# Seven low-half subtractions per token span placed elsewhere in VectorE's order

## The chip, the cores and the metric

The kernel runs on one core of a Trainium2 chip. The metric is device time in microseconds (us) of one execution; the time before is the median of three runs. The engines are called as in the profile: PE (TensorE), DVE (VectorE), ACT (ScalarE), POOL (GpSimd), SP (SyncE, which issues most DMAs). PEld is PE's weight load.

## The reference, cut to what matters

The input is 4 sequences of 3008 tokens of 256 numbers. A two-dimensional Fourier transform is taken of each, its real part is kept, and two feed-forward layers follow:

```
x = fft(fft(x, axis=1), axis=2).real      # (12032, 256)
h = x @ w_in1 ; x = relu(h)**2 @ w_out1   # 256 -> 2048 -> 256
h = x @ w_in2 ; y = (h * cos(h)) @ w_out2 # 256 -> 2048 -> 256
```

All is wanted in float32 precision, so each operand of a product is kept as two parts, a rounded high half and the low half that is left (value minus high half), and a product is three matmuls: low weight by high token, high weight by low token, high by high.

## The kernel before, in words

The Fourier transform and layer 1 fill the first 880 us or so; the change does not touch them. Layer 2 follows, and is cut into 12 spans of token pairs (`SPANS`, L45; index k), 11 of 512 columns and a last one of 388. For each span there are 8 steps (`NS`, L673; index i), each of which makes two of the 16 groups of 128 hidden units and adds what they give to the output.

**Operands of the first product.** It is done as a two by two block product with seven multiplications instead of eight. So each span needs seven token operands, named at L679: B11, B22 and B21 are columns of the layer's input as loaded; T1X, T2X, T3X and T4X are differences of such columns, made in place by `diff` (L691, on POOL for every span but the first). For each operand `x_hi` (L696, ACT) writes the rounded high half and `x_lo` (L702, DVE) the low half: one subtraction of 128x512 with both inputs in SBUF, listed by the profile at L704. The seven operands of span k are prepared while span k-1 is computed, and are kept in ten rotating buffers.

**One step.** The seven products M1 to M7 (L706) of three matmuls each go to two accumulation banks. M1, M6, M7 and M4 use bank 0, M5, M3 and M2 bank 1. Between them, sums are taken out: M1's result is copied by ACT (x1, L730), then M6 is added to the bank, that sum is copied by DVE (x2, L732), then M7 is added, and so on; so M6 must wait until x1 has read the bank, and M7 until x2 has. The corners C11, C12, C22 (DVE, listed at L237) and C21 (ACT, L742) make the hidden values h of the two groups. For each group j of the two: n (ACT, L747) rounds h to whole turns into the bank pp, r (DVE, L751) takes the rest, c (ACT, L757) the cosine, g (first group on DVE, second on POOL at L762) multiplies by h, `l2_hi` (ACT, L768) makes the high half and `l2_lo` (POOL, L773) the low half of the result. Then the 24 matmuls of the second product (m0 to m7, L785) add them to the output. Both n write the same bank pp, so n2 waits until r1 has read it.

**The order** is written out by hand. Every piece is given a time by `at` (L81), all pieces are sorted by it, and the sorted list is issued; each engine then runs its own part of the list strictly in that order. The unit of the table `OFF` (L983) is a step: the pieces of step i of a span stand at i + OFF, so a fraction tells the place within a step. By these numbers DVE's order within every step is r2 (.177), x2 (.362), C12 (.447), g1 (.513), C11 (.635), C22 (.701), x5 (.827), r1 (.893), and POOL's is l2 (.075), a `diff` where there is one (.5), g2 (.567), l1 (.818). PE's M3 stands at .133, M6 at .267, M7 at .467. ACT's n2 is at .052, x1 at .154, c1 at .321.

The lists `hi`, `lo` and `dif` (L994 to L996) give the places of the operands of span k, counted in steps of span k-1: for instance B11's low half at 3.76 stands in step 3 between C22 and x5. The first span's operands have a list of their own (L998 to L1002).

A step is told in the prediction by M3's start; it is recognised in the trace as the first of the three matmuls `b<-x,wel` of a step (M3, M6, M7 in this order).

Of the kernel before, what the change touches and what calls it, by code (L numbers as in the profile page):

```python
# [74 lines left out]
class Order:  # L75
# [5 lines left out]
    def at(self, t, fn, name=None):  # L81
        self.ops.append((TIMES.get(name, t), len(self.ops), fn))
# [12 lines left out]
def kernel(ctx: ExitStack, tc: tile.TileContext, x, x128, cs, tab0, tab1, w_in1, w_out1, w_in2, w_out2, out):  # L95
# [583 lines left out]
    T1X, B11, B22, T2X, T3X, B21, T4X = range(7)  # L679

    def load_o(k):
        c, w = SPANS[k]
        o_in[k] = [buf(t, "oin") for t in ("A0", "A1")]
        for t, o in zip(o_in[k], o_dram):
            nc.sync.dma_start(out=t[:, :, :w], in_=o[:, :, c:c + w])
# [5 lines left out]
    def diff(k, j, e):  # L691

        a, b = {T1X: ("b12", B11), T3X: (B22, "b12"), T2X: (B22, T1X), T4X: (B21, T2X)}[j]
        e.tensor_tensor(out=cols_of(k, j), in0=cols_of(k, a), in1=cols_of(k, b), op=ALU.subtract)

    def x_hi(k, j):  # L696
        tag = XTAGS[(7 * k + j) % 10]
        x = buf(tag, "x", F32R, late["pool"] if tag in ("cv", "xc") else work, XTAGS.count(tag))[:, :, :SPANS[k][1]]
        right[k, j] = x
        nc.scalar.activation(x[:, 0], cols_of(k, j), AF.Copy)  # L700

    def x_lo(k, j):  # L702
        x = right[k, j]
        nc.vector.tensor_tensor(out=x[:, 1], in0=cols_of(k, j), in1=f32(x)[:, 0], op=ALU.subtract)  # L704
# [3 lines left out]
    def product(k, i, b, pair_of, start):  # L708
        w = SPANS[k][1]
        j, r = pair_of  # L710
        (wh, wl), x = left(j, i), right[k, r]
        for q, (st, mv) in enumerate(((wl, 0), (wh, 1), (wh, 0))):
            nc.tensor.matmul(bank["b"][b][:, :w], st, x[:, mv], start=start and q == 0, stop=q == 2, skip_group_check=True)  # L713
# [4 lines left out]
    def ends(k, i):  # L718
        return k == len(SPANS) - 1 and i == NS - 1

    def copy_of(k, i, x, b, e):
        w = SPANS[k][1]
        if x == 5:
            u = buf("mid", "x5", F32, late["pool"], 2, (P, BLK)) if k == i == 0 else buf("u2", "x5", shape=(P, BLK))
        else:
            u = buf("zb", "x", bufs=2, shape=(P, BLK))
        us[k, i, x] = u = u[:, :w]
        src = bank["b"][b][:, :w]
        if e is nc.scalar:
            nc.scalar.activation(u, src, AF.Copy)  # L730
        else:
            nc.vector.tensor_copy(u, src)  # L732
# [6 lines left out]
    def corner(k, i, j, n, b, x):  # L739
        src, dst = bank["b"][b][:, :SPANS[k][1]], h_of(k, i, j)[:, n]  # L740
        if x is None:
            nc.scalar.activation(dst, src, AF.Copy)  # L742
        else:
            tt(dst, src, us[k, i, x], ALU.add)
# [25 lines left out]
    def l2_lo(k, i, j):  # L770
        hi, r = gs[2, k, i, j], rs.pop((k, i, j))
        lo = (buf("B1", "gl", F32R) if j and i % 2 else gl_buf())[:, :, :SPANS[k][1]]
        (V if ends(k, i) else G).tensor_tensor(out=lo, in0=r, in1=f32(hi), op=ALU.subtract)  # L773
        gs[2, k, i, j] = hi, lo

    def l2_mm2(k, i, n):
        m, j, half = n // 4, n // 2 % 2, n % 2
        w = SPANS[k][1]
        if i == 0 and j == half == 0:
            accs[2, k, m] = ps_a.tile([P, 2, BLK], F32, name=f"acc{m}")  # L780
        f = 2 * i + j
        hi, lo = gs[2, k, i, j]
        for q in range(3 * half, 3 * half + 3):
            part, g = ((0, hi), (1, hi), (0, lo))[q // 2]
            nc.tensor.matmul(accs[2, k, m][:, q % 2, :w], w_out_t([c[part] for c in wo2], f, m), g[:, q % 2],  # L785
                             start=f == 0 and q < 2, stop=f == NF - 1 and q >= 4)

    def l2_out(k, m):
        c, w = SPANS[k]
        a = accs.pop((2, k, m))[:, :, :w]  # L790
        last = k == len(SPANS) - 1
        o = buf("A0" if last and m else "B0", "y")[:, :, :w]
        dst = out[m].rearrange("p (n w) -> p n w", n=2)[:, :, c:c + w]
        if last:
            nc.scalar.activation(o[:, 0], a[:, 0], AF.Copy, scale=2.0 * math.pi)
            o2 = buf("zb", "y", bufs=2, shape=(P, BLK))[:, :w]
            nc.vector.tensor_scalar(out=o2, in0=a[:, 1], scalar1=2.0 * math.pi, scalar2=None, op0=ALU.mult)
            nc.scalar.dma_start(out=dst[:, 0], in_=o[:, 0])
            nc.sync.dma_start(out=dst[:, 1], in_=o2)
            return  # L800
        if m == 0:
            nc.scalar.activation(o, a, AF.Copy, scale=2.0 * math.pi)
        else:
            nc.vector.tensor_scalar(out=o, in0=a, scalar1=2.0 * math.pi, scalar2=None, op0=ALU.mult)
        nc.sync.dma_start(out=dst, in_=o)
# [183 lines left out]
    for k in range(len(SPANS)):  # L989
        base = L2S + STEP * NS * k  # L990
        if k:
            prev = base - STEP * NS
            at(prev + 2.1 * STEP, lambda k=k: load_o(k))
            hi = {B11: 2.82, B22: 3.82, T1X: 4.82, T2X: 6.82, T3X: 7.3, B21: 7.82, T4X: 8.3}  # L994
            lo = {B11: 3.76, B22: 4.76, T1X: 5.76, T2X: 7.32, T3X: 7.76, B21: 8.32, T4X: 8.34}
            dif = {T1X: 4.5, T3X: 5.5, T2X: 6.5, T4X: 7.5}  # L996
            t = {j: [prev + STEP * v[j] if j in v else None for v in (dif, hi, lo)] for j in range(7)}
        else:  # L998
            at(T2S - 13, lambda k=k: load_o(k))
            hi = {B11: 0, B22: 1, T1X: 2, T3X: 3, T2X: 4, B21: 5, T4X: 6}  # L1000
            dif = {T1X: 1, T3X: 2, T2X: 3, T4X: 4}
            t = {j: [T2S - 9.53 + dif.get(j, 0), T2S - 9.55 + hi[j], T2S - 8.55 + hi[j]] for j in range(7)}  # L1002
        for j in range(7):
            if j in dif:
                at(t[j][0], lambda k=k, j=j: diff(k, j, G if k else V))
            at(t[j][1], lambda k=k, j=j: x_hi(k, j))
            at(t[j][2], lambda k=k, j=j: x_lo(k, j))
        for i in range(NS):
            ops = {"M1": lambda k, i: product(k, i, 0, M1, True), "M6": lambda k, i: product(k, i, 0, M6, False),
                   "M7": lambda k, i: product(k, i, 0, M7, False), "M4": lambda k, i: product(k, i, 0, M4, False),  # L1010
                   "M5": lambda k, i: product(k, i, 1, M5, True), "M3": lambda k, i: product(k, i, 1, M3, False),
                   "M2": lambda k, i: product(k, i, 1, M2, True),
                   "x1": lambda k, i: copy_of(k, i, 1, 0, A), "x2": lambda k, i: copy_of(k, i, 2, 0, V),
                   "x5": lambda k, i: copy_of(k, i, 5, 1, V),
                   "C11": lambda k, i: corner(k, i, 0, 0, 1, 1), "C12": lambda k, i: corner(k, i, 0, 1, 1, 2),
                   "C21": lambda k, i: corner(k, i, 1, 0, 0, None), "C22": lambda k, i: corner(k, i, 1, 1, 0, 5)}
            for j in range(2):
                for n, fn in (("n", l2_n), ("r", l2_r), ("c", l2_cos), ("g", l2_g), ("h", l2_hi)):
                    ops[f"{n}{j + 1}"] = lambda k, i, j=j, fn=fn: fn(k, i, j)
                ops[f"l{j + 1}"] = lambda k, i, j=j: l2_lo(k, i, j)  # L1020
            for n in range(8):
                ops[f"m{n}"] = lambda k, i, n=n: l2_mm2(k, i, n)
            for name, fn in ops.items():
                off = END.get(name, OFF[name]) if ends(k, i) else OFF[name]
                at(base + STEP * (i + off), lambda k=k, i=i, fn=fn: fn(k, i), (name, k, i))
        for m, n in ((0, "m3"), (1, "m7")):
            off = END[n] if k == len(SPANS) - 1 else OFF[n]
            at(base + STEP * (NS - 1 + off + 0.09), lambda k=k, m=m: l2_out(k, m))
# [117 lines left out]
```

## Time and profile before

| what | value |
|---|---|
| median of 3 runs | 1907.06 us (1906.25 to 1907.62) |
| the profiled execution, its own time | 1904.97 us |
| its span (first to last instruction) | 1902.9 us |
| PE busy | 1836.1 us, 96% |
| DVE, ACT, POOL busy | 1454.8, 1443.0, 1374.1 us (76%, 76%, 72%) |
| mean granted TensorE clock | 0.996 of full speed |

What lies around the span is 2 us, and the profiled execution is 2 us below the median. Busy shares are averages over stages that differ. In layer 2 PE is the engine with the least idle time, so the way to read it is PE's order in time: how long a step takes, which steps take longer than others, and what PE waited for in those.

### The profile page before, as it was taken

To read this page: it belongs to the slowest core of one execution; us is meant where nothing else is said; L and a number is where in the kernel's file an instruction comes from. 1 tells how busy PE (TensorE), PEld (TensorE's weight loads), DVE (VectorE), ACT (ScalarE), POOL (GpSimd) and SP (SyncE) were. 2 spreads that over 40 slices of the span, in tenths; PEclk is the share of its full clock that TensorE was granted. 3 is DMA by queue.
4 is the path that set the end of the run, shared out by engine and by line. 5 is a ranking of instruction groups with operands and counts; after the bars stand their busy time and mean duration, and the time that the engine had idled before them with its cause. 6 is when DMAs were issued, how large, how long until landed. Compare 5 with 4: busy or idle time off the path is not lost.

```text
span 1902.9 us, 23618 instructions
## 1 busy us (share of the span) xinstructions
PE 1836.1 (96%) x8256; PEld 1507.2 (79%) x8256; DVE 1454.8 (76%) x1867; ACT 1443.0 (76%) x1618; POOL 1374.1 (72%) x1144
## 2 busy tenths in 40 slices
PE   6899999999999999999999999999999999999998
PEld 3678787788888888887777777787777777787788
DVE  6889958768578886776777787877777777777775
ACT  3788777878788988887777777777777777777776
POOL 1567777778777778776768786777777777777775
PEclk9899999999999999999999999999999999999999
DMA  8563434244243343442110101010010101010000
GB/s 281 179 248 107 148 117 149 104 142 147 96 124 117 104 137 105 121 149 90 65 45 1 44 1 45 1 45 21 24 45 1 45 1 45 0 45 28 12 23 17
DMA packets 72410, 153.17 MB, mean 80 GB/s; under 512 B 8304, under 2 KB 31872, under 8 KB 72196
## 3 DMA queue, kind: packets, MB, share of 16 engines
q1 hardware_dynamic: 69732, 143.46, 22.7%
q0 software_dynamic: 1840, 6.73, 1.2%
q8 instruction: 64, 1.05, 0.2%
q10 hardware_dynamic: 720, 1.50, 0.2%
q14 instruction: 54, 0.44, 0.1%
HBM read 105.20 MB, written 51.09 MB: 82 GB/s over the span
## 4 chain that ended last, share of the span: by engine, by line
PE 63%; DVE 8%; issue 5%; ACT 3%; POOL 3%; DVEq 0%; ACTq 0%; POOLq 0%
PE b L713 18%; PE acc L785 18%; PE acc L644 18%; PE h L602 8%; DVE r L751 3%; DVE h L237 2%; POOL gl L773 2%; ACT pp L747 2%; DVE x L732 1%; PE h L335 1%; DVE x L704 1%; POOL r L762 1%; ACT x L730 1%; DVE s L237 0%; DVE u L609 0%
## 5 line engine op out<-in xcount | busy, mean ns | idle before, releaser
L632 POOL TENSOR_TENSOR gl<-s,gh 128x256 fp32r<-128x256 f32 (+2 forms) x768 | 601.3, 815 | 211.7 <-ACT gh L622 169.5
L773 POOL TENSOR_TENSOR gl<-r,gh 128x1024 fp32r<-128x1024 f32 (+1 forms) x190 | 454.1, 2396 | 58.8 <-ACT gh L768 57.7
L762 POOL TENSOR_TENSOR r<-r,h 128x1024 f32<-128x1024 f32 (+1 forms) x95 | 225.3, 2372 | 204.1 <-ACT r L757 183.5
L751 DVE SCALAR_TENSOR_TENSOR r<-pp,h 128x1024 f32<-128x1024 int32 (+1 forms) x192 | 229.5, 1195 | 112.4 <-ACT pp L747 108.7
L619 ACT ACTIVATE s<-s 128x1024 f32<-128x1024 f32 (+2 forms) x192 | 199.7, 1040 | 86.4 <-DVE s L237 82.1
L785 PE MATMUL acc<-gh,wbl 128*128 128x512 f32 (+1 forms) x768 | 264.7, 385 | 0.0
L768 ACT ACTIVATE gh<-r 128x1024 fp32r<-128x1024 f32 (+1 forms) x192 | 200.0, 1042 | 82.8 <-DVE r L237 82.7
L237 DVE TENSOR_TENSOR s<-u,h 128x512 f32<-128x512 f32 (+2 forms) x380 | 240.0, 673 | 25.0 <-POOL gl L632 3.5
L644 PE MATMUL acc<-gh,wbh 128*128 128x512 f32 (+2 forms) x768 | 236.9, 390 | 0.7 <-DVE o L669 0.7
L644 PE MATMUL acc<-gl,wbh 128*128 128x512 f32 (+2 forms) x768 | 235.4, 387 | 1.5 <-POOL gl L632 1.3
L785 PE MATMUL acc<-gh,wbh 128*128 128x512 f32 (+1 forms) x768 | 233.8, 385 | 1.0 <-ACT gh L768 1.0
L644 PE MATMUL acc<-gh,wbl 128*128 128x512 f32 (+2 forms) x768 | 234.4, 386 | 0.0
L785 PE MATMUL acc<-gl,wbh 128*128 128x512 f32 (+1 forms) x768 | 233.5, 385 | 0.4 <-POOL gl L773 0.4
L713 PE MATMUL b<-x,wah 128*128 128x512 f32 (+1 forms) x768 | 233.6, 385 | 0.0
L747 ACT ACTIVATE pp<-h 128x1024 int32<-128x1024 f32 (+1 forms) x192 | 192.1, 1000 | 52.3 <-DVE r L751 50.2
L609 DVE SCALAR_TENSOR_TENSOR u<-zb,wc,h 128x512 f32<-128x512 f32 (+2 forms) x190 | 138.9, 731 | 95.7 <-PE h L602 94.9
L622 ACT ACTIVATE gh<-s 128x1024 fp32r<-128x1024 f32 (+2 forms) x192 | 201.0, 1047 | 6.1
L620 ACT ACTIVATE s<-s 128x1024 f32<-128x1024 f32 (+2 forms) x192 | 200.9, 1046 | 6.1
L237 DVE TENSOR_TENSOR h<-b,x 128x512 f32<-128x512 f32 (+1 forms) x288 | 187.0, 677 | 18.7 <-PE b L713 15.0
L732 DVE COPY x<-b 128x512 f32<-128x512 f32 (+1 forms) x192 | 129.9, 676 | 84.7 <-PE b L713 84.6
L713 PE MATMUL b<-x,weh 128*128 128x512 f32 (+1 forms) x576 | 175.5, 386 | 0.0
L757 ACT ACTIVATE pp<-r,halfpi 128x1024 f32<-128x1024 f32 (+1 forms) x96 | 106.1, 1105 | 83.0 <-DVE r L751 83.0
(145 smaller groups left out, 3420.7 us busy)
## 6 DMA issues: line engine op xcount, KB each, us to landing
oin<-o SPq DMA_DIRECT2D x22, 512.0 KB, 5.2
y_out<-y SPq DMA_DIRECT2D x22, 512.0 KB, 3.1
inT<-x_in SPq DMA_DIRECT2D x18, 512.0 KB, 8.6
o<-o SPq DMA_DIRECT2D x16, 512.0 KB, 3.7
mid<-w_in SPq DMA_DIRECT2D x14, 511.5 KB, 5.8
mid<-w_out SPq DMA_DIRECT2D x14, 511.0 KB, 4.3
t<-tab SPq DMA_DIRECT2D x9, 756.0 KB, 4.4
t<-tab SPq DMA_DIRECT2D x9, 752.0 KB, 6.9
```

The source lines that it names most:

```text
L237: nc.vector.tensor_tensor(out=out, in0=in0, in1=in1, op=op)
L620: nc.scalar.activation(s[:, :, :w], s[:, :, :w], AF.Square)
L622: nc.scalar.activation(hi[:, :, :w], s[:, :, :w], AF.Copy)
L632: nc.gpsimd.tensor_tensor(out=lo[:, n, cols], in0=s[:, n, cols], in1=f32(hi)[:, n, cols], op=ALU.subtract)
L644: nc.tensor.matmul(accs[1, k][m][:, n, :w], wt, g[:, n, :w], start=begin and i == 0, stop=end and i == 2)
L713: nc.tensor.matmul(bank["b"][b][:, :w], st, x[:, mv], start=start and q == 0, stop=q == 2, skip_group_check=True)
L747: nc.scalar.activation(bank["p"].bitcast(I32)[:, :, :SPANS[k][1]], hs[k, i, j], AF.Copy, bias=0.25)
L751: nc.vector.scalar_tensor_tensor(out=r, in0=bank["p"].bitcast(I32)[:, :, :SPANS[k][1]], scalar=-1.0, in1=hs[k, i, j], op0=ALU.mult, op1=AL ...
L762: (V if ends(k, i) else G).tensor_tensor(out=r, in0=r, in1=h, op=ALU.mult)
L768: nc.scalar.activation(hi, rs[k, i, j], AF.Copy)
L773: (V if ends(k, i) else G).tensor_tensor(out=lo, in0=r, in1=f32(hi), op=ALU.subtract)
L785: nc.tensor.matmul(accs[2, k, m][:, q % 2, :w], w_out_t([c[part] for c in wo2], f, m), g[:, q % 2], start=f == 0 and q < 2, stop=f == NF - ...
```

## The change

One line of the table of places is replaced: that of the low halves of the operands of span 1 and later. No instruction is added or removed, and no size, buffer or transfer is changed.

```diff
             hi = {B11: 2.82, B22: 3.82, T1X: 4.82, T2X: 6.82, T3X: 7.3, B21: 7.82, T4X: 8.3}
-            lo = {B11: 3.76, B22: 4.76, T1X: 5.76, T2X: 7.32, T3X: 7.76, B21: 8.32, T4X: 8.34}
+            lo = {B11: 3.34, B22: 4.34, T1X: 5.34, T2X: 7.34, T3X: 7.96, B21: 8.34, T4X: 8.35}
             dif = {T1X: 4.5, T3X: 5.5, T2X: 6.5, T4X: 7.5}
```

## Rows read from the trace of the kernel before

**Rows 1.** The page's part on engines: busy us, share of the span, instructions.
```profile
PE 1836.1 (96%) x8256; PEld 1507.2 (79%) x8256; DVE 1454.8 (76%) x1867; ACT 1443.0 (76%) x1618; POOL 1374.1 (72%) x1144
```

**Rows 2.** Waits of PE, 915 to 1830 us: releaser, total us, times, longest.
```profile
PE b L713 <- ACT x L730: 19.4, 32, 0.6
PE b L713 <- DVE x L732: 2.9, 11, 0.3
```

**Rows 3.** Timeline of PE, some starts: start us, us, instruction [idle before <-releaser].
```profile
1004.16 0.39 PE L713 MATMUL b<-x,wel 128*128 128x512 f32 x1
...
1014.36 0.39 PE L713 MATMUL b<-x,wel 128*128 128x512 f32 x1
...
1016.50 0.50 PE L713 MATMUL b<-x,wel 128*128 128x512 f32 x1 [0.62 <-ACT x L730]
...
1025.49 0.39 PE L713 MATMUL b<-x,wel 128*128 128x512 f32 x1
...
1057.01 0.39 PE L713 MATMUL b<-x,wel 128*128 128x512 f32 x1
...
1059.15 0.50 PE L713 MATMUL b<-x,wel 128*128 128x512 f32 x1 [0.62 <-ACT x L730]
...
1068.76 0.39 PE L713 MATMUL b<-x,wel 128*128 128x512 f32 x1
```

**Rows 4.** Timelines of POOL and DVE around three low halves in the places of before.
```profile
1010.12 2.40 POOL L773 TENSOR_TENSOR gl<-r,gh 128x1024 fp32r<-128x1024 f32 x1
...
1010.32 2.75 DVE L704 TENSOR_TENSOR x<-oin,x 128x512 fp32r<-128x512 f32 x1
...
1021.45 1.07 DVE L704 TENSOR_TENSOR x<-oin,x 128x512 fp32r<-128x512 f32 x1
...
1265.42 0.74 DVE L704 TENSOR_TENSOR x<-oin,x 128x512 fp32r<-128x512 f32 x1
```

**Rows 5.** The chain that ended last, 1013 to 1017 us: start us, us, what.
```profile
1013.00 0.68 DVE x L732
1013.67 1.14 DVE r L751
...
1014.90 1.03 ACT pp L747
1015.93 0.52 ACT x L730
...
1016.50 0.96 PE b L713 x3
```

**Rows 6.** Timelines of DVE, POOL and ACT, 1296 to 1304 us, between two even steps.
```profile
1298.39 1.21 DVE L751 SCALAR_TENSOR_TENSOR r<-pp,h 128x1024 f32<-128x1024 int32 x1
1301.03 1.22 DVE L751 SCALAR_TENSOR_TENSOR r<-pp,h 128x1024 f32<-128x1024 int32 x1 [1.42 <-ACT pp L747]
1302.17 0.88 DVE L704 TENSOR_TENSOR x<-oin,x 128x512 fp32r<-128x512 f32 x1
1303.22 0.69 DVE L732 COPY x<-b 128x512 f32<-128x512 f32 x1 [0.17 <-PE b L713]
...
1296.75 2.40 POOL L773 TENSOR_TENSOR gl<-r,gh 128x1024 fp32r<-128x1024 f32 x1
1300.09 2.42 POOL L773 TENSOR_TENSOR gl<-r,gh 128x1024 fp32r<-128x1024 f32 x1 [0.94 <-ACT gh L768]
1302.46 1.75 POOL L694 TENSOR_TENSOR oin<-oin 128x512 f32<-128x512 f32 x1
...
1299.91 1.02 ACT L747 ACTIVATE pp<-h 128x1024 int32<-128x1024 f32 x1
```

**Rows 7.** Timeline of DVE: x2 of two steps, and two low halves in a row.
```profile
1017.50 0.69 DVE L732 COPY x<-b 128x512 f32<-128x512 f32 x1 [0.24 <-PE b L713]
...
1059.82 1.28 DVE L704 TENSOR_TENSOR x<-oin,x 128x512 fp32r<-128x512 f32 x2
1061.02 0.68 DVE L732 COPY x<-b 128x512 f32<-128x512 f32 x1
```

## The prediction

> **What bounds the kernel now.** I read the engines' busy times first: PE is busy 96% of the span, the others about three quarters [rows 1]. So only time in which PE stands still can be won. Next, PE's waits in layer 2 from the point where the moved instructions begin: M6 waited for x1 (ACT's copy of M1) 32 times, 19.4 us, and M7 for x2 (DVE's copy) 11 times, 2.9 us [rows 2]. Nothing else shows there. What such a wait costs is read from step lengths, since a stopped PE also starts again more slowly. Step 3 of this span, from M3 to M3, takes 1014.36 - 1004.16 = 10.20 us without a wait; step 4, whose M6 waited 0.62 us, takes 1025.49 - 1014.36 = 11.13 us [rows 3]. So one M6 stall costs 0.93 us, not 0.62. Step 0 of the next span, in which M6 and then M7 waited, takes 1068.76 - 1057.01 = 11.75 us [rows 3]: 0.62 us more.
>
> Why M6 waits is in the chain of work that ended last. It runs x5, r1, n2, x1, M6 with no gap to speak of: DVE's copy at 1013.00, r1 at 1013.67, ACT's n2 at 1014.90, x1 at 1015.93, PE at 1016.50 [rows 5]. In front of that x5 stands B11's low half. It takes 2.75 us, from 1010.32 to 1013.07, and POOL had begun a subtraction of 2.40 us at 1010.12, 0.20 us earlier [rows 4]. That one ended at 1012.52; the low half ended 0.55 us later. Its work is therefore about 0.6 us, and the other 2.2 us is standing still behind POOL. Where POOL did not stand in the way, the same instruction took 0.74 us [rows 4].
>
> The low half of B22 in the next step takes 1.07 us [rows 4] and no M6 stall follows. In all, 32 low halves of 2.6 to 2.75 us stand in the trace of DVE from 915 us on (three per span for 11 spans, less one), and as many M6 waits [rows 2]: one for one. In the span in which B11 took 0.74 us [rows 4], no wait follows it.
>
> The Trainium skill ("SBUF — State Buffer", section "SBUF: two separate sides") says that VectorE and GpSimd share a pair of ports, which an instruction of either holds to its end; for VectorE that holds for instructions with two SBUF inputs. The trace agrees: 2.75 us is POOL's remainder plus 0.55.
>
> **What the change does, part by part.** No work is added or removed, and `x_lo` issues no DMA, so no queue is touched.
>
> T2X (7.32 to 7.34), B21 (8.32 to 8.34) and T4X (8.34 to 8.35): no other DVE piece stands between old and new place (r2 is at .177, x2 at .362). DVE's order is the same, so these 33 of the 77 cost nothing by themselves.
>
> B11, B22 and T1X go from behind C22 to between r2 and x2, 33 instructions. The trace already has an instruction in that place: T2X. In the one span where it follows a step without a wait, r2 starts at 1301.03 and T2X at 1302.17, taking 0.88 us; x2 behind it still waits 0.17 us for PE [rows 6]. POOL is not idle there: its l2 runs from 1300.09 to 1302.51 [rows 6]. But only the last 0.3 us of it are left when DVE arrives, against 2.2 us in the old place. So the price in the new place is zero as long as x2 is not late, and what is queued behind is x2, then C12 and g1; M7 waits for x2. How late x2 may be is worked out from step 0: there x2 starts 1061.02 - 1059.15 = 1.87 us after M6, and in step 4 1017.50 - 1016.50 = 1.00 us after it, when only PE held it [rows 3, 7]. It was 0.87 us late and that cost 0.62 us, so 0.25 us are free. Bounds for one such place: nothing below, since x2 cannot go before PE is done; above, a full block as in the old place, ending 2.75 us after 1302.17, which makes x2 1.7 us late. I take zero, from the nearest row, T2X.
>
> With these three gone from the old place, x5 waits only for PE, r1 is early, and n2 starts when ACT is free. The even step shows it: r1 is done at 1299.60 and n2 starts at 1299.91 without a wait [rows 6].
>
> T3X goes from 7.76 to 7.96, between r1 and r2, 11 instructions. In the even step r1 ends at 1299.60, POOL's l1 ended at 1299.15 and its l2 starts at 1300.09, after 0.94 us in which POOL waited for ACT; r2 starts at 1301.03, after 1.42 us of waiting for n2 [rows 6]. A low half of 0.6 to 0.7 us fits: from 1299.6 to 1300.2. It may hold l2 back by 0.1 us. Above, the bound is a block by the whole of l2 (a rival below). I take zero on DVE.
>
> Step 0, with B21 and T4X in a row before x2: today r2 of that step is late because of T3X, and both take 1.28 us unblocked [rows 7]. Afterwards r2 ends at the even step's time and they meet the end of l2. l2 then ends at about 1302.6; B21 ends 0.54 us behind it (as T2X did: 1303.05 against 1302.51 [rows 6]), T4X 0.6 us later, at 1303.75, where x2 could have started at 1303.22. So x2 is some 0.55 us late, 0.25 are free, and the step pays about 0.3 us instead of today's 0.62. Bounds: nothing, or today's 0.62.
>
> **The sum.** 32 M6 stalls x 0.93 = 29.8 us, and 11 x (0.62 - 0.3) = 3.5 us: 33 us in all. Against the profiled execution's 1904.97 us that is 1872; the median of the runs is 2 us above that execution, so I say **1874 us**. If every stall went, it would be 29.8 + 11 x 0.62 = 36.6 us, or 1870.5. That is the floor: every step then takes 10.20 us, the time of its 45 matmuls.
>
> **Rivals.**
>
> *POOL's difference goes first.* At 4.5 and 5.5 POOL has a `diff` queued right behind l2, at the very place where B22 and T1X now wait. If it takes the ports, the low half waits another 1.2 us (the `diff` of 1.75 us at 1302.46 was itself held 0.54 us by T2X [rows 6]), x2 is 1.0 us late and 22 steps pay 0.75 us: 17 us back, 1891. Against it: T2X stands before the `diff` of T4X in the same way, and DVE went first. By the Trainium skill (the same section) whoever starts first holds the ports; it does not say who is served first of two that wait.
>
> *T3X is caught by l2.* If l1 ends after 1300, l2 starts at once and T3X waits for it until 1303.05; r2 ends at 1304.3, then the two low halves, so x2 starts 2.3 us late and the step pays 2.05 us instead of 0.3: 11 x 1.75 = 19 us back, 1893. Against it: the 0.94 us in which POOL waits for ACT [rows 6].
>
> *The stall stays or moves.* If n2 or x1 were held by something else as soon as r1 is early, most of the gain would be missing: about 1905. Against it stand the even steps. That the change doesn't do what it says belongs here: POOL is not idle at .34, only nearly done.
>
> *Slower.* POOL needs some 8.5 of each 10.20 us (2.41 for g2, 2.4 each for l1 and l2, 1.3 for a `diff`). If, in steps that follow each other without stalls, its l2 came to start after r2's end, 2.1 us later than in rows 6, every low half before x2 would stand a full 2.75 us: x2 1.7 us late, 1.45 us paid, 33 times, 48 us; step 0 pays 1.4 us more than today, 15 us; less the 30 won, that is 33 us slower, 1940. It decides from a low half of some 2.2 us on, where 33 late x2 cost what 32 stalls do. Against it: l2's start is set by ACT's high half, not by POOL's backlog [rows 6].
>
> **How the numbers follow.** Forecast 0.77, `diff` first 0.08, T3X caught 0.06, stall stays 0.05, slower 0.04. From the floor to the second rival is 0.91; the range 1870 to 1893 takes in these cases and leaves 0.09 out. Without the two rivals the forecast's own range is 1870 to 1878. A difference of 0.2% (3.8 us) is about what a measurement of this kernel can tell from none. Faster by more than that: the first three cases and a part of the fourth, 0.93; within it 0.03; slower 0.04.
>
> **What would show it.** Right: low halves of at most about 1.1 us each; no M6 wait on ACT's copy; steps of 10.20 us, 10.5 for step 0; M7's wait on x2 shorter than 0.3 us; `diff` some 0.5 us longer behind B22 and T1X. Wrong: low halves of 2 us or more in their new places, x2 without a wait for PE in front of it, M7 waits in steps 3 to 5, or r2 late in step 0.

## The result and the profile after

The changed kernel took 1871.24 us, the median of 4 runs (1870.84 to 1872.39), against 1906.65 us for the kernel before, the median of its 4 runs (1904.18 to 1907.62). The ratio is 0.9817, with a 95% interval of 0.98 to 0.9834: 1.8% or 35.4 us faster. The forecast was 1874 us, the range 1870 to 1893.

The page's first lines, on the span and on the engines, of the changed kernel:

```profile
span 1870.6 us, 23619 instructions
...
PE 1828.6 (98%) x8256; PEld 1513.5 (81%) x8256; DVE 1400.0 (75%) x1867; ACT 1437.0 (77%) x1618; POOL 1379.5 (74%) x1144
```

Against [rows 1] DVE is busy 55 us less with the same number of instructions, and POOL 5 us more. The same stretch of layer 2 as in [rows 2], 915 to 1830 us, has no wait of PE left; the busy times up to 1800 us say the same (window, its length, then busy us of PE, PEld, DVE, ACT and POOL with their instructions, granted clock of PE, DMA share, GB/s):

```profile
915.00:1800.00 885.00, 885.00 (x3905) 730.71 (x3905) 658.97 (x782) 671.97 (x782) 694.72 (x305) 1.00 0.08 26
```

PE is busy for all 885 us. The groups of the moved instruction and of POOL's differences in layer 2, those of 512 columns (line, operation and shape, count, busy us, mean ns, idle before), first in the kernel before:

```profile
L704 DVE TENSOR_TENSOR x<-oin,x 128x512 fp32r<-128x512 f32 x70 | 112.6, 1621 | 0.0
L694 POOL TENSOR_TENSOR oin<-oin 128x512 f32<-128x512 f32 x40 | 56.2, 1406 | 0.0
```

and then in the changed kernel:

```profile
L694 POOL TENSOR_TENSOR oin<-oin 128x512 f32<-128x512 f32 x40 | 65.5, 1637 | 0.0
L704 DVE TENSOR_TENSOR x<-oin,x 128x512 fp32r<-128x512 f32 x70 | 58.6, 848 | 0.0
```

A low half takes 848 ns in the mean where it took 1621. POOL's differences take 231 ns more each: part of the waiting has gone over to POOL, where it holds up nothing that PE waits for.

The timelines of the changed kernel over steps 7 and 0 (PE, then DVE, then POOL), which answer to [rows 3, 6, 7]:

```profile
1044.39 0.39 PE L713 MATMUL b<-x,wel 128*128 128x512 f32 x1
1045.75 0.39 PE L713 MATMUL b<-x,wel 128*128 128x512 f32 x1
...
1054.59 0.39 PE L713 MATMUL b<-x,wel 128*128 128x512 f32 x1
1055.95 0.39 PE L713 MATMUL b<-x,wel 128*128 128x512 f32 x1
...
1064.87 0.39 PE L713 MATMUL b<-x,wel 128*128 128x512 f32 x1
...
1045.57 0.87 DVE L704 TENSOR_TENSOR x<-oin,x 128x512 fp32r<-128x512 f32 x1
1046.62 0.69 DVE L732 COPY x<-b 128x512 f32<-128x512 f32 x1 [0.18 <-PE b L713]
...
1051.99 1.21 DVE L751 SCALAR_TENSOR_TENSOR r<-pp,h 128x1024 f32<-128x1024 int32 x1
1053.12 0.68 DVE L704 TENSOR_TENSOR x<-oin,x 128x512 fp32r<-128x512 f32 x1
1054.63 1.22 DVE L751 SCALAR_TENSOR_TENSOR r<-pp,h 128x1024 f32<-128x1024 int32 x1 [0.82 <-ACT pp L747]
1055.77 1.48 DVE L704 TENSOR_TENSOR x<-oin,x 128x512 fp32r<-128x512 f32 x2
1057.17 0.68 DVE L732 COPY x<-b 128x512 f32<-128x512 f32 x1
...
1050.35 2.42 POOL L773 TENSOR_TENSOR gl<-r,gh 128x1024 fp32r<-128x1024 f32 x1
1053.69 2.41 POOL L773 TENSOR_TENSOR gl<-r,gh 128x1024 fp32r<-128x1024 f32 x1 [0.93 <-ACT gh L768]
```

Step 7 takes 1054.59 - 1044.39 = 10.20 us, step 0 takes 1064.87 - 1054.59 = 10.28 us instead of 11.75 [rows 3]. T3X's low half at 1053.12 takes 0.68 us. POOL's l2 starts at 1053.69, 0.11 us before the recorded end of that low half, and takes its usual 2.41 us, so neither holds up the other; r2 comes when ACT lets it. The two low halves at 1055.77 make x2 start 1.22 us after M6, where it starts 0.87 us after it in step 7.

Where the time came from is counted in layer 2 itself: from M3 of step 3 of the first span to M3 of step 6 of the last one. Kernel before, PE's timeline:

```profile
919.13 0.39 PE L713 MATMUL b<-x,wel 128*128 128x512 f32 x1
...
1872.73 0.34 PE L713 MATMUL b<-x,wel 128*128 128x388 f32 x1
```

and the changed kernel:

```profile
921.85 0.39 PE L713 MATMUL b<-x,wel 128*128 128x512 f32 x1
...
1840.44 0.34 PE L713 MATMUL b<-x,wel 128*128 128x388 f32 x1
```

953.60 us against 918.59 us: 35.0 of the 35.4 us by which the medians differ. The spans of the two profiled executions differ by 32.3 us only, since that of the changed kernel reaches this stretch 2.7 us later (921.85 against 919.13); the change touches nothing before it.

### The profile page after: what moved, and what is told of

Read it like the earlier page. It is cut to its first block, busy times and chain, and to the rows that moved or that the text cites. A ratio compares the mean times of both kernels' runs of the same rounds, so it can differ in the third digit from the quotient of the medians.

```text
span 1870.6 us, 23619 instructions
## 1 busy us (share of the span) xinstructions
PE 1828.6 (98%) x8256; PEld 1513.5 (81%) x8256; DVE 1400.0 (75%) x1867; ACT 1437.0 (77%) x1618; POOL 1379.5 (74%) x1144
## 3 DMA queue, kind: packets, MB, share of 16 engines
q0 software_dynamic: 1840, 6.73, 1.2%
## 4 chain that ended last, share of the span: by engine, by line
PE 79%; DVE 2%; ACT 1%; issue 0%; ACTq 0%; DVEq 0%
PE acc L785 27%; PE b L713 24%; PE acc L644 18%; PE h L602 9%; PE h L335 1%; DVE s L237 0%; DVE u L609 0%; DVE inT L237 0%; DVE r L751 0%; ACT o L668 0%; ACT pp L747 0%; DVE ws L237 0%; DVE wf L237 0%; DVE h L237 0%; PE pp L602 0%
## 5 line engine op out<-in xcount | busy, mean ns | idle before, releaser
L644 PEld LDWEIGHTS acc<-gl,wbh 128*128 128x128 f32 x768 | 144.7, 188 | 31.3 <-POOL gl L632 3.4
```

The lines of the kernel that those rows point to most:

```text
L644: nc.tensor.matmul(accs[1, k][m][:, n, :w], wt, g[:, n, :w], start=begin and i == 0, stop=end and i == 2)
```

## The experiments

The theory: a low half that meets a running subtraction of POOL stands until that one ends, so x5, r1, n2, x1 and M6 are late, and the change takes the low halves out of that meeting. The rivals: it is only their place in DVE's order, whatever POOL does; or only some of the moves count.

**Each part alone.** `e1_t3x_back` is the changed kernel with T3X's low half in its old place:

```diff
-            lo = {..., T2X: 7.34, T3X: 7.96, ...}
+            lo = {..., T2X: 7.34, T3X: 7.76, ...}
```

> The changed kernel with T3X's low half back at 7.76; B11, B22 and T1X stay in their new places. Theory (a low half that starts behind POOL's l1 stands about 2.2 us, x5, r1, n2, x1 and M6 are late by it, one M6 stall costs 0.93 us and makes step 0 pay 0.62 us more): T3X's low half takes 2.75 us, all others at most 1.1 us; 11 M6 waits of 0.62 us; step 0 takes 11.75 us again, against 10.29 us in the changed kernel; 11 x 1.46 = 16 us over the changed kernel, 1887 us. Rival (each moved low half brings its share by its own 0.6 us of DVE time, whatever POOL does): a quarter of the gain is lost, about 9 us, 1880 us. Rival (only the first three matter, T3X's new place brings nothing): 1871 us.

It took 1886.19 us (ratio to the kernel before 0.9903, interval 0.9886 to 0.9919), 15.0 us over the changed kernel. Its PE waits, 915 to 1840 us, and its PE timeline in step 0:

```profile
PE b L713 <- ACT x L730: 6.8, 11, 0.6
PE b L713 <- DVE x L732: 2.6, 10, 0.3
```

```profile
1054.07 0.39 PE L713 MATMUL b<-x,wel 128*128 128x512 f32 x1
1056.21 0.50 PE L713 MATMUL b<-x,wel 128*128 128x512 f32 x1 [0.61 <-ACT x L730]
1058.82 0.50 PE L713 MATMUL b<-x,wel 128*128 128x512 f32 x1 [0.28 <-DVE x L732]
1065.80 0.39 PE L713 MATMUL b<-x,wel 128*128 128x512 f32 x1
```

11 M6 waits, step 0 of 11.73 us, and no wait in any other step from step 3 of the first span on: the theory's numbers, and neither rival's.

`e2_t3x_only` is the kernel before with that one low half moved:

```diff
-            lo = {..., T2X: 7.32, T3X: 7.76, ...}
+            lo = {..., T2X: 7.32, T3X: 7.96, ...}
```

> The kernel before with T3X's low half alone moved to 7.96. Theory: 21 of the 32 M6 waits stay (those behind B11 and T1X), those of step 0 go, and with them its longer M7 wait; 16 us under the kernel before, 1890.5 us, and the two parts of the change add up: this gain and that of the other three together make the whole 35 us. Rival (the stalls are linked, so that taking one out of a span moves POOL's subtractions into the way of others, as in the one span of the trace before where B22 was blocked instead of B11 and T1X): the number of blocked low halves per span stays 3 or changes to other operands, and the gain is under 10 us.

It took 1889.28 us (ratio 0.9918, interval 0.9904 to 0.9933), 16.0 us under the kernel before on the same chip (1905.29). The PE wait left in it:

```profile
PE b L713 <- ACT x L730: 12.6, 21, 0.6
```

21 waits, as expected, and no M7 wait. The parts add up: T3X 16.0 us here, the other three 1905.29 - 1886.19 = 19.1 us, together 35.1 of the 35.4 us.

**Is it POOL, or the place?** In `e3_l1_memset` nothing is moved; POOL's l1 is replaced.

```diff
-        (V if ends(k, i) else G).tensor_tensor(out=lo, in0=r, in1=f32(hi), op=ALU.subtract)
+        if j or ends(k, i):
+            (V if ends(k, i) else G).tensor_tensor(out=lo, in0=r, in1=f32(hi), op=ALU.subtract)
+        else:
+            G.memset(f32(lo), 0.0)
```

> The kernel before, all low halves in their places of before, but POOL's l1 (low half of the first group's result, two inputs read from SBUF) is a memset of the same tile; the output lacks that low half. Theory (the low half stands because POOL's instruction reads SBUF beside it): low halves in the old places of 0.6 to 0.8 us, no M6 wait behind them, layer 2's steps 10.2 to 10.3 us, about 1871 to 1874 us with nothing moved. Rival (any POOL instruction holds the ports to its end, a writing one too): the low half lasts until the memset ends and 0.55 us more, so what is left of the stall goes with the memset's length. Rival (it is the place in DVE's order, not POOL): M6 waits of 0.6 us stay, 1905 us.

It took 1869.7 us, one run, with all low halves in their old places, and its layer 2 has no PE wait. POOL's memset and the low half of B11, from the timelines of POOL and DVE:

```profile
1006.10 0.96 POOL L776 MEMSET gl<- 128x1024 f32 x1
...
1006.42 0.68 DVE L704 TENSOR_TENSOR x<-oin,x 128x512 fp32r<-128x512 f32 x1
```

The low half starts 0.32 us into the memset and still takes 0.68 us. So the place alone costs nothing, and it matters what POOL does: a subtraction that reads two tiles stops the low half [rows 4], a memset that reads nothing does not. The Trainium skill ("SBUF — State Buffer", section "SBUF: two separate sides") has a VectorE instruction with two SBUF inputs held up only by a GpSimd instruction that reads SBUF; this run agrees, with 0.68 us.

The other half of the question is what DVE does. `e8_copy` keeps POOL and all places of the kernel before, and makes the low half a copy with one input:

```diff
-        nc.vector.tensor_tensor(out=x[:, 1], in0=cols_of(k, j), in1=f32(x)[:, 0], op=ALU.subtract)
+        if k:
+            nc.vector.tensor_copy(x[:, 1], cols_of(k, j))
+        else:
+            nc.vector.tensor_tensor(out=x[:, 1], in0=cols_of(k, j), in1=f32(x)[:, 0], op=ALU.subtract)
```

> The kernel before, all places as before, but the low half of the operands of span 1 and later is a copy of the column (one input from SBUF) instead of the subtraction of the high half (two inputs); the output lacks the right low halves. Theory (it is the second input that DVE and POOL share): copies of 0.7 us at most in the old places, no M6 wait, about 1871 to 1874 us. Rival (a copy from SBUF to SBUF takes the shared ports as well): the copies in step 3, 5 and 7 end 0.3 to 0.6 us after POOL's l1, 2.4 us or more, the M6 waits stay, about 1900 us.

1889.62 us, one run: the rival was right about the stall, though its time, about 1900 us, was 10 us too high. The timelines of POOL and DVE around B11's copy, and the waits of PE from 915 to 1840 us (the added lines shift the line numbers by 3):

```profile
1008.23 2.41 POOL L776 TENSOR_TENSOR gl<-r,gh 128x1024 fp32r<-128x1024 f32 x1
...
1008.44 2.48 DVE L705 CAST x<-oin 128x512 fp32r<-128x512 f32 x1
...
PE b L716 <- ACT x L733: 11.1, 32, 0.4
```

The copy ends 0.28 us after POOL's l1; the subtraction ended 0.55 us after it. It works faster, and it stands behind POOL just as long. All 32 M6 waits are there; a stalled step takes some 10.85 us instead of 11.13, since x5 comes 0.27 us earlier. A second input is not needed for the stall, then; whether the subtraction itself stands because of its second input, this run does not tell. The same section of the Trainium skill names, beside instructions with two SBUF inputs, VectorE's 2-port performance mode as a holder of the shared ports. The run fits that, with 2.48 us; that the copy ran in such a mode is not shown.

**How many fit in front of x2?** `e4_repeat` is the changed kernel with B22's low half twice and T1X's three times:

```diff
+            for _ in range({B22: 2, T1X: 3}.get(j, 1) if k else 1):
-            at(t[j][2], lambda k=k, j=j: x_lo(k, j))
+                at(t[j][2], lambda k=k, j=j: x_lo(k, j))
```

> The changed kernel with the low half of B22 issued twice in a row (step 4) and that of T1X three times (step 5); step 3 keeps one. It measures how late x2 may be. Theory (x2 has slack behind one low half; in step 0 of the changed kernel two in a row made x2 start 1.22 us after M6 instead of 0.87, and the step paid 0.09 us): step 3 10.20 us, step 4 with two like step 0, 10.29 us, step 5 with three has x2 another 0.62 us later and pays 0.7 us, 10.9 us; over 11 spans about 8.5 us, 1880 us. Rival (the forecast's slack of 0.25 us for a lateness of x2 against its start in a step without any low half): step 4 pays 0.3 us, step 5 0.9 us, 13 us in all, 1884 us. Rival (DVE has slack for all of it): 10.20 us each, 1871 us.

It took 1936.4 us, one run: 65 us over the changed kernel and 31 over the kernel before. All three expectations fell. DVE's and POOL's timelines in steps 4 and 5:

```profile
1107.67 2.57 DVE L704 TENSOR_TENSOR x<-oin,x 128x512 fp32r<-128x512 f32 x2
1110.16 0.68 DVE L732 COPY x<-b 128x512 f32<-128x512 f32 x1
...
1119.11 5.34 DVE L704 TENSOR_TENSOR x<-oin,x 128x512 fp32r<-128x512 f32 x3
...
1105.58 2.40 POOL L773 TENSOR_TENSOR gl<-r,gh 128x1024 fp32r<-128x1024 f32 x1 [0.93 <-ACT gh L768]
1107.94 1.75 POOL L694 TENSOR_TENSOR oin<-oin 128x512 f32<-128x512 f32 x1
...
1121.49 2.40 POOL L762 TENSOR_TENSOR r<-r,h 128x1024 f32<-128x1024 f32 x1 [0.34 <-ACT r L757]
```

The first low half waits for l2 (which ends at 1107.98) and gets in before the difference that POOL has queued: 0.87 us, as in step 7 of the changed kernel. Then the difference runs until 1109.69, and the second low half ends 0.55 us after that, at 1110.24. In step 5 the third one stands behind POOL's g2 as well, which ends at 1123.89; it ends at 1124.45. In the ten spans whose low halves have 512 columns, step 4 takes 11.4 us and step 5 14.1 to 16.7 us.

Not all of step 5 is waiting. PE stands still for 3.6 us before M7. In eight of the ten spans its granted clock falls to 0.50, the lower of its two levels (1.2 instead of 2.4 GHz), about the end of that wait, and stays there for 3 to 7 us; those steps take 15.7 to 16.7 us. In the other two the clock stays at 1.00, and the step takes 14.1 to 14.2 us. Step 5 of two spans, and 1 us within the first of them (columns as above, the granted clock is the third number from the end):

```profile
1029.38:1045.15 15.77, 12.18 (x47) 9.42 (x45) 11.86 (x11) 7.17 (x9) 8.87 (x5) 0.89 0.00 1
1117.92:1132.08 14.16, 10.54 (x47) 8.29 (x46) 11.86 (x11) 7.16 (x9) 8.93 (x5) 1.00 0.00 0
1039.00:1040.00 1.00, 1.00 (x4) 0.81 (x3) 0.56 (x1) 1.00 (x2) 0.50 (x1) 0.50 0.00 0
```

`e7_dif_away` asks whether it is that queued difference. B22 and T1X twice each; in step 5 the difference stands behind g2, at 5.7:

```diff
-            dif = {T1X: 4.5, T3X: 5.5, T2X: 6.5, T4X: 7.5}
+            dif = {T1X: 4.5, T3X: 5.7, T2X: 6.5, T4X: 7.5}
...
+            for _ in range(2 if k and j in (B22, T1X) else 1):
-            at(t[j][2], lambda k=k, j=j: x_lo(k, j))
+                at(t[j][2], lambda k=k, j=j: x_lo(k, j))
```

> The changed kernel with the low halves of B22 (step 4) and of T1X (step 5) issued twice, and the difference T3X, which POOL has queued behind l2 in step 5, moved behind g2 (5.7); the difference T1X of step 4 stays behind l2. It asks why the repeats cost 1.2 us and 5 us per step where the two low halves of step 0 cost 0.09. Theory (whoever came first is served: a second low half stands behind the difference that has waited since l2's end): step 4 11.4 us as before, its two low halves 2.57 us together; step 5 10.3 us, its two 1.48 us together, as in step 0. Rival (it is the number of low halves in front of x2, not POOL's queue): steps 4 and 5 alike, 11.4 us each.

1886.04 us, one run. The two pairs in DVE's timeline:

```profile
1097.97 2.58 DVE L704 TENSOR_TENSOR x<-oin,x 128x512 fp32r<-128x512 f32 x2
...
1109.37 1.61 DVE L704 TENSOR_TENSOR x<-oin,x 128x512 fp32r<-128x512 f32 x2
1110.90 0.68 DVE L732 COPY x<-b 128x512 f32<-128x512 f32 x1
```

With the difference in line the pair takes 2.58 us and the step 11.4; with it away 1.61 us and 10.42. The theory holds, and the number of low halves is not the reason: the one that has waited goes before the one that comes next. (Strict turns between the two engines would look the same here.) Step 5 pays 0.2 us rather than 0.1, since its pair ends 0.13 us later than that of step 0.

**A smaller dose.** `e5_before_r1` puts three low halves between x5 and r1:

```diff
-            lo = {B11: 3.34, B22: 4.34, T1X: 5.34, ...}
+            lo = {B11: 3.85, B22: 4.85, T1X: 5.85, ...}
```

> The changed kernel with the low halves of B11, B22 and T1X between x5 and r1 (3.85, 4.85, 5.85), T3X as changed. A smaller dose of the old stall. Theory (what a stall costs is set by how late r1 and so n2 are): in an even step x5 ends at 1041.88 and POOL's l1 at 1042.56, so the low half takes some 1.3 us and r1 ends 1.2 us later, of which the 0.3 us in which n2 does not wait for r1 are free; n2 and x1 are then 0.9 us late. In the kernel before r1 was 1.84 us later than in an even step and a stall cost 0.93 us, so 0.9 us of lateness of r1 are free, and 1.2 us cost 0.3: steps of 10.5 us, 33 x 0.3 = 10 us, 1881 us. Rival (the price is the low half's own 0.6 us, whatever it waits for, and r1 has that free): 10.20 us, 1871 us. Rival (any wait behind POOL costs the whole stall): 1902 us.

1897.01 us, one run, 16 us more than the theory said. Its first stalled step is as expected: the low half takes 1.32 us and step 4 10.53 us (forecast 1.3 and 10.5). Steps 5 and 6 take 11.2 us. DVE's and POOL's timelines, steps 3 to 5:

```profile
1096.14 1.32 DVE L704 TENSOR_TENSOR x<-oin,x 128x512 fp32r<-128x512 f32 x1
...
1106.67 2.00 DVE L704 TENSOR_TENSOR x<-oin,x 128x512 fp32r<-128x512 f32 x1
...
1094.50 2.41 POOL L773 TENSOR_TENSOR gl<-r,gh 128x1024 fp32r<-128x1024 f32 x1
...
1105.71 2.41 POOL L773 TENSOR_TENSOR gl<-r,gh 128x1024 fp32r<-128x1024 f32 x1
```

The first stall makes r2, the cosines and POOL's g2 behind them late, so POOL's l1 begins 11.21 us after the one of the step before while DVE's low half follows after 10.53. The next low half meets 1.45 us of l1 where the first met 0.77, and takes 2.0 us. A stall is handed on to the next step; the expectation took the steps one by one.

**More of them in the idle time of POOL.** `e6_idle_only` puts B11, B22, T1X and T2X, like T3X, between r1 and r2, and takes T4X out of the pair in front of x2:

```diff
-            lo = {B11: 3.34, B22: 4.34, T1X: 5.34, T2X: 7.34, T3X: 7.96, B21: 8.34, T4X: 8.35}
+            lo = {B11: 3.96, B22: 4.96, T1X: 5.96, T2X: 6.96, T3X: 7.96, B21: 8.34, T4X: 8.48}
```

> The changed kernel with B11, B22, T1X and T2X too between r1 and r2 (3.96 to 6.96), where POOL stands idle, and T4X between C12 and g1 (8.48); B21 alone stays in front of x2. Theory: low halves of 0.68 us in the first four places, no difference of POOL held up (1.28 us each instead of 1.75), x2 of step 0 no longer late, step 0 10.20 instead of 10.29 us: 11 x 0.09 = 1 us under the changed kernel, 1870 us, which the times can hardly tell; the trace can. Rival (T4X holds g1 up by 0.65 us, and with it ACT's high half and POOL's l1): step 0 of 10.3 us or more, 1872 us or above.

1870.44 us (ratio 0.9812, interval 0.9795 to 0.9828): not to be told from the changed kernel. The low halves between r1 and r2 take 0.68 us, as expected, POOL's differences 1.28 us, and x2 is on time in step 0. But step 0 takes 10.24 to 10.31 us all the same. From the timelines of PE's weight loads, DVE and POOL there, where M3 starts at 1053.84:

```profile
1059.87 0.19 PEld L713 LDWEIGHTS b<-x,wal 128*128 128x128 f32 x1 [0.18 <-DVE h L237]
...
1057.41 0.68 DVE L704 TENSOR_TENSOR x<-oin,x 128x512 fp32r<-128x512 f32 x1
...
1057.41 2.96 POOL L762 TENSOR_TENSOR r<-r,h 128x1024 f32<-128x1024 f32 x1 [2.06 <-ACT r L757]
```

T4X's low half makes g1 and the corner C11 behind it late, and the next M5 waits for C11. The same low half meets POOL's g2, which takes 2.96 us instead of 2.41. So the rival had step 0 about right, with T4X as the cause, but PE's wait came through C11, which it did not name; and the cost is as small as that of the late x2, so the 1872 us or more did not come.

## Why the prediction was right, point by point

*What bounds the kernel, and the price of a stall.* Right. 32 M6 waits at 0.93 us were the larger term of the sum (29.8 us), and steps 4 and 6 went from 11.13 to 10.20 us, the whole of the price. Reading it from step lengths mattered: the idle time shown with the waits is 19.4 us [rows 2], and 35 us were won. The reason given for 0.93 against 0.62 us, a slower start of PE, is half of it. In the stalled step M6 starts 2.14 us after M3 [rows 3], in step 7 above 1.36: that is 0.78 us later, not 0.62, because idle time is counted from the recorded end of the matmul before, and a matmul recorded with 0.39 us is followed by the next after 0.23 us (45 of them in 10.20 us). The other 0.15 us are lost behind M6, whose first matmul takes 0.50 us.

*Three entries that leave DVE's order as it was.* Right: T2X takes 0.87 us (0.88 in [rows 6]), and B21 with T4X stay in a row.

*B11, B22 and T1X in front of x2.* Right at zero: 0.74 to 1.12 us each, and steps 3 to 5 take 10.20 us. In steps 4 and 5 x2 still waits some 0.18 us for PE. In step 3 nothing is left of that wait, though x2 is on time: POOL has no idle time before the l2 in front of B11, which starts 0.2 to 0.3 us later against M3 than the others do, and B11's low half takes 1.12 us in most spans. The forecast had not foreseen that; the spare time of x2 happened to cover it. The free time of x2, put at 0.25 us, is borne out by the steps in which it was used up: x2 0.35 us late in step 0 cost 0.08 us, 0.48 us late in `e7_dif_away` cost 0.22, 1.45 us late in step 4 of `e4_repeat` cost some 1.2. That is 0.2 to 0.3 us free each time.

*T3X between r1 and r2.* Right: 0.68 us, and l2 starts on time at 1053.69 (I had allowed for 0.1 us of delay).

*Step 0.* The mechanism was right and the term too small: 11 x (0.62 - 0.3) = 3.5 us was forecast, 11 x (0.62 - 0.08) = 5.9 us came. The step of the working that was off is x2's lateness, 0.35 us and not 0.55. I had let l2 end 0.1 us later than it does, and counted x2 from the recorded end of the low half in front, though x2's start lies 0.08 us before it. This is most of what separates 1874 from 1871.24; the rest is that the kernel before ran some tenths faster in these runs than in those shown.

*Rivals.* "POOL's difference goes first" did not happen in the changed kernel, since one low half in front of each x2 has waited longer than the difference. `e4_repeat` and `e7_dif_away` show that the mechanism is real one instruction later. "T3X is caught by l2" did not happen: l1 had ended at 1052.77 and l2 began at 1053.69. "The stall stays" did not. "Slower" did not: POOL's l2 follows ACT's high half with 0.93 us of idle time before it in steps 4 to 7 and 0, as the argument against it said. In step 3 that argument fails, since POOL's own backlog sets l2's start there, but by 0.2 to 0.3 us only. That a crowded place in front of x2 can make the kernel slower than before is what `e4_repeat` shows, by another way than the one that I priced.

## What to carry to other kernels

Here an elementwise instruction that took up to four times its usual length on one shape (2.75 us against 0.68) was standing, not working. Where two lengths show up for one shape, look which instruction of the other engine began just before it and ended just before its end. With VectorE and GpSimd both on SBUF operands, ask of each place in a hand-written order not whether GpSimd is idle there but how much of its running instruction is left and what it has queued next: one VectorE instruction at the tail of it cost nothing here; a second one cost 0.1 to 0.2 us per step where nothing was queued, and 1.2 us where a difference was. Price a stall by the length of the step around it, and expect it to shift the other engine's work against the next step.

## What the runs showed of the hardware that was not expected

A copy from SBUF with one input stands behind POOL as long as a subtraction with two: it took 2.48 us, where two unblocked ones in a row took 0.75 us, so its work is some 0.37 us by estimate. POOL's memset of 128x1024 took 0.96 us and ran beside a low half of 0.68 us without either being longer. And the recorded time of a POOL instruction includes its waiting: its differences are listed with 1.75 us where a low half went first, 1.28 us where none did.
